# Reordering the second batch of an attention-and-MLP kernel: loads as k, q, v; k pooled apart from v; folded blocks 3 and 4 made inside its first product

## The chip, the cores and the metric

The kernel runs on one core of a Trainium2 chip. The metric is the device time of one execution in microseconds (us). The profile's span is 1.8 us shorter than that time (248.5 against 250.3 us for the kernel before). Engines are called by their names in the profile: PE is TensorE, DVE is VectorE, ACT is ScalarE, POOL is GpSimd, SP is SyncE; PEld is TensorE's weight loads, and a q behind a name (SPq, POOLq) is the engine's own queue of issues and waits. PSUM is the memory into which TensorE's products go; an *eviction* is the DVE or ACT instruction that takes a result out of it. A run of a program on one core is counted as fast unless it is over 1.5% above the fastest of its kernel.

## The reference

Batch 8, 8 heads of width 64, sequence 576, 32 memory slots, then a feed-forward layer of 512 to 2048 to 512. Cut to what matters:

```python
a   = softmax(phi, axis=2)                       # over the sequence
k_m = einsum('bhsm,bhsd->bhmd', a, k)            # "pooling": 32 rows per head
v_m = einsum('bhsm,bhsd->bhmd', a, v)
attn = softmax(q @ k_m.T / 8)                    # [576, 32] per head
x    = concat_heads(attn @ v_m)                  # [8, 576, 512]
xn   = (x - mean) / sqrt(var + 1e-6) * g_ln
out  = x + relu(xn @ w_ch1) @ w_ch2
```

## The kernel before

Batches are numbered 0 to 7; the "second batch" is batch 1. The kernel never multiplies x by w_ch1. It folds the pooled v into w_ch1, giving the *folded blocks* w1b (four blocks of 512 columns per batch), and multiplies those by the normalised attention Eh. In the text folded blocks are counted from 1 (block 3 is `a_w1b(b, 2)`), the 16 column blocks of the product from 0, as in the code. That multiplication is the *first product* (`mm1`). The *second product* (`mm2`) applies w_ch2.

```python
def kv_mm(b, ps, sl, js=range(4)):       # pooling: 2 x 4 x 9 small matmuls, k and v side by side
    for c in range(NS):
        for j in js:
            for g in range(2):
                nc.tensor.matmul(ps[32*j:32*(j+1), g, 0:D*(sl.stop-sl.start)],
                                 e[r:r+TS, c, j, :], kv[r:r+TS, j, sl, D*c:D*(c+1)], ...)

def a_w1b(b, n, part=None):              # folded block n
    ps = big([P, 2, 512], FP32, "w1b_ps")            # one of three double PSUM buffers
    ...                                              # 8 matmuls, 64*32 each
    for g in range(2):                               # two evictions on DVE, 128x512 fp32
        nc.vector.scalar_tensor_tensor(out=s["w1b"][:, g, fs], in0=m_sb[:, fs],
            scalar=s["rsum"][:, g:g+1], in1=ps[:, g, 0:N], op0=ALU.mult, op1=ALU.add)

def mm1(b, j0, j1):                      # first product; column block j needs folded block j // 4
    for j in range(j0, j1):
        h_ps = big([P, 2, 512], FP32, "h_ps")        # the same three buffers
        ...                                          # 4 matmuls of 288 columns
        if j % 3 or j == 0: nc.scalar.activation(out=dst, in_=h_ps[...], func=AF.Relu)
        else:               nc.vector.tensor_scalar(out=dst, in0=h_ps[...], ... op0=ALU.max)
```

The order of every engine's work is that of the Python text, as the timelines show (their lines: start, length, engine, line, operation, shapes, count, and in brackets the idle time before it with what ended it). The second batch's attention is interleaved with the second product of tiles 2 and 3 of the first pair of batches:

```python
    mm2(0, 2, 0, 8)
    a_kv(1)                              # k and v pooled together
    mm2(0, 2, 8, 12)
    a_tr(1)                              # transposes of pooled k and v
    a_qT(1, 0)                           # transposes of q
    a_w1b(1, 0)
    mm2(0, 2, 12, 16, finish=False)
    a_qT(1, 1)
    a_w1b(1, 1)
    a_sc(1)                              # scores
    mm2_out(0, 2)
    mm2(0, 3, 0, 4)
    a_w1b(1, 2)
    a_den(1)                             # denominators and Eh
    load(2); a_exp(2)
    mm2(0, 3, 4, 12)
    a_w1b(1, 3)
    mm2(0, 3, 12, 16, finish=False)
    a_vb(1)
    mm2_out(0, 3)
    ... # then, per batch: mm1(b, 0, 16), and the next batch's attention between mm2s
```

The softmax here doesn't subtract the row's maximum and nothing guards it: scores larger than these inputs give would overflow.

Of the kernel before, what the change touches and what calls it, by code (L numbers as in the profile page):

```python
# [9 lines left out]
FP32 = mybir.dt.float32  # L10
BF16 = mybir.dt.bfloat16
# [5 lines left out]
def kernel(  # L17
# [11 lines left out]
    nc = tc.nc  # L29

    B, H, S, D = q.shape
# [3 lines left out]
    P = 128  # L35
    TS = 64
    NS = S // TS
# [18 lines left out]
    def big(shape, dtype, name):  # L56
        return psum.tile(shape, dtype, name=name, tag="big", bufs=3)
# [16 lines left out]
    def rows(src, b):  # L74
        return src[b].rearrange("(j e) (p c) d -> (e p) j (c d)", e=2, p=TS)

    def halves(two):
        return (slice(0, 2), slice(2, 4)) if two else (slice(0, 4),)

    def load_kv(b):  # L80
        t = inp.tile([P, 4, 2, NS * D], BF16, name="kv_bf")
        for slot, src in ((0, k), (1, v)):
            for js in halves(b < 1):
                nc.gpsimd.dma_start(out=t[:, js, slot, :], in_=rows(src, b)[:, js, :])  # L84
        return t

    def load_q(b):
        t = inp.tile([P, 4, NP, P], BF16, name="q_bf")
        pad = nc.vector if b == 0 else nc.gpsimd
        pad.memset(t[:, :, NP - 1, D:], 0.0)  # L90
        for js in halves(b < 2):
            nc.gpsimd.dma_start(out=t.rearrange("p j n x -> p j (n x)")[:, js, 0:NS * D],  # L92
                                in_=rows(q, b)[:, js, :])
        return t
# [43 lines left out]
    for n in range(4):  # L138
        w2_load(n)
    phi1 = load_phi(1, nc.gpsimd)  # L140
    kv1 = load_kv(1)
    q1 = load_q(1)
    loaded[1] = (phi1, kv1, q1)

    g_bf = consts.tile([P, 4], BF16, name="g_bf")
# [94 lines left out]
    def a_kv(b):  # L240
        ps = big([P, 2, 512], FP32, "kv_ps")
        if b < 2:
            kv_sum(b, ps)
        else:

            for i in range(2):
                nc.tensor.matmul(ps[:, 0, P:P + 2], st8[b]["es"][:, i, :], ones8,
                                 start=(i == 0), stop=(i == 1))
        kv_mm(b, ps, slice(0, 2))
        k_out(b, ps, b < 2)  # L250
        v_out(b, ps[:, :, D:2 * D])
        rs_out(b, ps)

    def a_tr(b, k_part=True, v_part=True):
        s = st8[b]
        t_ps = big([P, 3, P], BF16, "kvT_ps")
        if k_part:
            kvT = att.tile([P, 3, P], BF16, name="kvT")
            s["kvT"] = kvT
            for g in range(2):  # L260
                nc.tensor.transpose(t_ps[:, g, :], s["k2"][:, g].rearrange("p a d -> p (a d)"), ident)
        kvT = s["kvT"]
        if v_part:
            nc.tensor.transpose(t_ps[:, 2, :], s["v2"].rearrange("p a d -> p (a d)"), ident)
        if k_part:
            nc.vector.tensor_copy(out=kvT[:, 0:2, :], in_=t_ps[:, 0:2, :])
        if v_part:
            nc.vector.tensor_tensor(out=kvT[:, 2, :].rearrange("p (j m) -> p j m", m=M),
                                    in0=t_ps[:, 2, :].rearrange("p (j m) -> p j m", m=M),
                                    in1=g_bf.unsqueeze(2).to_broadcast([P, 4, M]), op=ALU.mult)  # L270
            rsum = att.tile([P, 2], FP32, name="rsum")
            nc.vector.tensor_reduce(out=rsum, in_=s["v2"], axis=mybir.AxisListType.X, op=ALU.add)
            s["rsum"] = rsum

    def a_vb(b):
        s = st8[b]
        vb = att.tile([P, 2, 4, D], BF16, name="vb", bufs=3)
        for g in range(2):
            vsl = s["v2"][:, g, :].unsqueeze(1).to_broadcast([P, 4, D])
            eng = nc.vector if b < 2 else nc.gpsimd  # L280
            eng.tensor_tensor(out=vb[:, g], in0=vsl, in1=vmask, op=ALU.mult)  # L281
        s["vb"] = vb
# [91 lines left out]
    def a_w1b(b, n, part=None):  # L374
        s = st8[b]
        if n == 0 and part in (None, 0):
            s["w1b"] = att.tile([P, 2, F], BF16, name="w1b", bufs=1)
        ps = big([P, 2, 512], FP32, "w1b_ps")
        fs = slice(512 * n, 512 * (n + 1)) if part is None else W1C[part]
        N = fs.stop - fs.start  # L380
        for j in range(4):
            for g in range(2):
                r = 64 * g
                nc.tensor.matmul(  # L384
                    ps[32 * j:32 * (j + 1), g, 0:N], s["kvT"][r:r + 64, 2, 32 * j:32 * (j + 1)],
                    w1r[r:r + 64, j, fs], start=True, stop=True, tile_position=(r, 32 * j))
        for g in range(2):
            nc.vector.scalar_tensor_tensor(  # L388
                out=s["w1b"][:, g, fs], in0=m_sb[:, fs], scalar=s["rsum"][:, g:g + 1],
                in1=ps[:, g, 0:N], op0=ALU.mult, op1=ALU.add)  # L390


    pair = {}

    def mm1(b, j0, j1):
        s = st8[b]
        if b % 2 == 0 and j0 == 0:
            pair[b // 2] = moe.tile([P, JC, 2 * S], BF16, name="rT", bufs=1)
        rT = pair[b // 2]
        off = S * (b % 2)  # L400
        for j in range(j0, j1):
            h_ps = big([P, 2, 512], FP32, "h_ps")
            for g in range(2):
                for half in range(2):
                    nc.tensor.matmul(  # L405
                        h_ps[:, half, 0:HS], s["w1b"][:, g, P * j:P * (j + 1)],
                        s["Eh"][:, g, HS * half:HS * (half + 1)],
                        start=(g == 0), stop=(g == 1))
            dst = rT[:, j, off:off + S].rearrange("p (a x) -> p a x", a=2)
            if j % 3 or j == 0:  # L410
                nc.scalar.activation(out=dst, in_=h_ps[:, :, 0:HS], func=AF.Relu)  # L411
            else:
                nc.vector.tensor_scalar(out=dst, in0=h_ps[:, :, 0:HS], scalar1=0.0, scalar2=None,  # L413
                                        op0=ALU.max)
# [53 lines left out]
    def mm2(pr, t, j0, j1, ps=None, finish=True):  # L468
        rT = pair[pr]
        if j0 == 0:  # L470
            chs[(pr, t)] = one([P, C], FP32, "ch_ps") if ps is None else ps
        ch_ps = chs[(pr, t)]
        for j in range(j0, j1):
            nc.tensor.matmul(ch_ps, rT[:, j, P * t:P * (t + 1)], w2b[:, j, :],  # L474
                             start=(j == 0), stop=(j == JC - 1))
        if j1 == JC and finish:
            mm2_out(pr, t)

    def mm2_last(pr, t):

        x, rstd = xs[(pr, t)]
        for n in range(2):
            ps = big([P, 2, 512], FP32, "last_ps")
            cs = slice(256 * n, 256 * (n + 1))
            for j in range(JC):
                nc.tensor.matmul(ps[:, 0, 0:256], pair[pr][:, j, P * t:P * (t + 1)], w2b[:, j, cs],  # L486
                                 start=(j == 0), stop=(j == JC - 1))
            nc.vector.scalar_tensor_tensor(out=x[:, cs], in0=ps[:, 0, 0:256], scalar=rstd,
                                           in1=x[:, cs], op0=ALU.mult, op1=ALU.add)
            for u, queue in ((0, nc.sync), (1, nc.scalar)):  # L490
                lo = P * t + TS * u
                dst = out[2 * pr + lo // S].rearrange("(p c) x -> c p x", c=NS)
                queue.dma_start(out=dst[CO[lo % S // TS]][:, cs], in_=x[TS * u:TS * (u + 1), cs])

    def mm2_out(pr, t):
        ch_ps = chs[(pr, t)]
        x, rstd = xs[(pr, t)]
        nc.vector.scalar_tensor_tensor(out=x, in0=ch_ps, scalar=rstd, in1=x,  # L498
                                       op0=ALU.mult, op1=ALU.add)
        for u in range(2):  # L500
            lo = P * t + TS * u
            dst = out[2 * pr + lo // S].rearrange("(p c) x -> c p x", c=NS)
            nc.sync.dma_start(out=dst[CO[lo % S // TS]], in_=x[TS * u:TS * (u + 1), :])
# [44 lines left out]
    w1_mean(4)  # L548
    m_copy(4)
    a_w1b(0, 3)  # L550
    a_vb(0)
    mm1(0, 8, 16)

    x_tiles(0, [0, 1])
    x_tiles(0, [2, 3])
# [4 lines left out]
    a_exp(1)  # L560
    mm2(0, 0, 4, 16)
    mm2(0, 1, 4, 16)
    mm2(0, 2, 0, 8)
    a_kv(1)
    mm2(0, 2, 8, 12)
    a_tr(1)
    a_qT(1, 0)
    a_w1b(1, 0)
    mm2(0, 2, 12, 16, finish=False)
    a_qT(1, 1)  # L570
    a_w1b(1, 1)
    a_sc(1)
    mm2_out(0, 2)
    mm2(0, 3, 0, 4)
    a_w1b(1, 2)
    a_den(1)
    load(2)
    a_exp(2)
    mm2(0, 3, 4, 12)
    a_w1b(1, 3)  # L580
    mm2(0, 3, 12, 16, finish=False)
    a_vb(1)
    mm2_out(0, 3)

    a_qT(2, 0)
    late = []
    for b in range(1, B):
        pr, nb = b // 2, b + 1
        odd = b % 2
# [125 lines left out]
```

## Time and profile before

| | before |
|---|---|
| time, median of 3 runs | 251.05 us (250.95 to 251.22) |
| span of the profiled execution | 248.5 us (its time 250.3) |
| PE busy | 96% of the span |
| first product of batch 0, first to last matmul | 19.55 to 33.53 us |
| first product of batch 1 | 53.34 to 61.93 us |
| first product of each later batch | 8.12 us |
| last tile of the second product to the end of the span | 7.45 us |

The prediction shows the lines that carry the argument. Two more are needed as a yardstick, from the TensorE timeline (start, length, engine, line, operation, shapes, count, and in brackets the idle time before it with what ended it):

```profile
53.34 1.21 PE L405 MATMUL h_ps<-Eh,w1b 128*128 128x288 bf16 x8
54.79 7.14 PE L405 MATMUL h_ps<-Eh,w1b 128*128 128x288 bf16 x56 [0.25 <-ACT rT L411]
```

In the kernel before, batch 1's first product has one short wait and then runs 56 matmuls without a gap. The next work starts at 61.77, so the product takes 8.43 us from start to start (8.59 to the modelled end of its last matmul).

### The profile page before, as it was taken

How to read it: one execution, taken by the hardware profiler on the slowest of the kernel's cores; microseconds unless marked ns; L12 is line 12 of the kernel's file. 1: busy time of each engine (PE TensorE's matmuls, PEld its weight loads, DVE VectorE, ACT ScalarE, POOL GpSimd, SP SyncE). 2: the span in 40 equal slices, each digit the busy share in tenths (PEclk: the TensorE clock that was granted, in tenths of full speed). 3: DMA queues.
4: the chain of work that ended last, by engine and by line, in shares of the span. 5: the costliest groups of instructions: out<-in, count | busy, mean ns of one | idle time of the engine just before them, and what ended most of it. 6: DMA issues, size and time to landing. Idle time of an engine off the chain costs nothing.

```text
span 248.5 us, 5893 instructions
## 1 busy us (share of the span) xinstructions
PE 238.5 (96%) x2491; PEld 132.5 (53%) x2491; DVE 156.2 (63%) x304; ACT 130.0 (52%) x219; POOL 60.6 (24%) x100
## 2 busy tenths in 40 slices
PE   7879999999999999999999999999999999999993
PEld 2444555557544665467544774467444764476453
DVE  3246663785578646686569547785679538783641
ACT  3165572587463555736472646655680755465210
POOL 8643241032515402090206202170205011000000
PEclk9999999999999999999999999999999999999999
DMA  7999999998599899829975995539983302103133
GB/s 151 195 202 207 206 257 208 291 222 148 119 200 210 122 218 242 160 38 201 251 127 112 158 245 136 122 38 223 209 158 77 80 7 46 42 17 70 42 84 84
DMA packets 42450, 36.82 MB, mean 148 GB/s; under 512 B 17460, under 2 KB 37688, under 8 KB 42424
## 3 DMA queue, kind: packets, MB, share of 16 engines
q0 software_dynamic: 17776, 19.53, 46.9%
q1 hardware_dynamic: 24488, 16.79, 29.3%
q8 instruction: 19, 0.31, 0.5%
q10 hardware_dynamic: 160, 0.13, 0.2%
q14 instruction: 7, 0.06, 0.1%
HBM read 41.42 MB, written 9.44 MB: 205 GB/s over the span
## 4 chain that ended last, share of the span: by engine, by line
PE 88%; DMA 4%; DVE 2%; ACT 2%; POOL 1%; issue 1%; DVEq 0%; POOLq 0%
PE ch_ps L474 50%; PE h_ps L405 25%; DMA kv_bf<-in_v_dram 4%; PE w1b_ps L384 3%; PE kv_ps L210 2%; PE o_ps L435 2%; PE last_ps L486 1%; PE sc_ps L322 1%; PE m_ps L165 1%; ACT rT L411 1%; PE den_ps L353 1%; DVE w1b L388 1%; POOL q_bf L92 1%; ACT E_sb L327 1%; POOL kv_bf L84 1%
## 5 line engine op out<-in xcount | busy, mean ns | idle before, releaser
L474 PE MATMUL ch_ps<-w2b,rT 128*128 128x512 bf16 x560 | 128.4, 380 | 0.0
L474 PEld LDWEIGHTS <-rT 128*128 128x128 bf16 x560 | 52.0, 98 | 63.5 <-issue 6.5
L405 PE MATMUL h_ps<-Eh,w1b 128*128 128x288 bf16 x512 | 66.6, 286 | 1.3 <-ACT rT L411 1.2
L411 ACT ACTIVATE rT<-h_ps 128x576 bf16<-128x576 f32 x88 | 52.4, 648 | 28.7 <-PE h_ps L405 28.7
L405 PEld LDWEIGHTS <-w1b 128*128 128x128 bf16 x512 | 49.5, 97 | 18.3 <-issue 2.6
L388 DVE SCALAR_TENSOR_TENSOR w1b<-m_sb,rsum,w1b_ps 128x512 bf16<-128x512 f32 (+1 forms) x66 | 44.2, 726 | 9.6 <-PE w1b_ps L384 5.3
L413 DVE TENSOR_SCALAR rT<-h_ps 128x576 bf16<-128x576 f32 x40 | 30.3, 757 | 24.9 <-PE h_ps L405 24.3
L498 DVE SCALAR_TENSOR_TENSOR x_sb<-ch_ps,rstd,x_sb 128x512 f32<-128x512 f32 x35 | 26.1, 746 | 9.9 <-PE ch_ps L474 9.1
L454 DVE BATCH_NORM_STATS2 bst<-x_sb 128x6 f32<-128x512 f32 x36 | 24.4, 678 | 7.6 <-ACT x_sb L441 7.6
L441 ACT ACTIVATE x_sb<-o_ps 128x1024 f32<-128x1024 f32 (+1 forms) x20 | 17.5, 938 | 18.4 <-PE o_ps L435 18.4
L281 POOL TENSOR_TENSOR vb<-v,vmask 128x256 bf16<-128x256 bf16 x12 | 7.7, 663 | 60.1 <-DVE rs L237 60.1
L194 POOL TENSOR_TENSOR es<-e_sb 128x512 f32<-128x512 bf16 x6 | 6.9, 1156 | 62.9 <-ACT e_sb L187 62.9
L460 ACT ACTIVATE rstd<-mv,eps_sb 128x2 f32<-128x2 f32 (+1 forms) x20 | 5.9, 297 | 30.4 <-DVE mv L455 30.2
L327 ACT ACTIVATE E_sb<-sc_ps,rs 128x640 bf16<-128x640 f32 x16 | 11.8, 790 | 12.4 <-PE sc_ps L322 12.4
L369 DVE SCALAR_TENSOR_TENSOR Eh<-E_sb,rs,rden 128x576 bf16<-128x576 bf16 x16 | 12.4, 815 | 8.8 <-ACT rden L368 8.8
L384 PE MATMUL w1b_ps<-w1r,kvT 64*32 64x512 bf16 (+1 forms) x264 | 10.9, 374 | 0.0
L179 PE MATMUL w_ps<-fill 128*128 128x512 f32 (+1 forms) x16 | 9.4, 699 | 1.6 <-DVE fill L119 1.6
L227 DVE CAST k<-kv_ps 128x256 bf16<-128x256 f32 x7 | 3.0, 425 | 12.5 <-PE kv_ps L210 12.5
L187 ACT ACTIVATE e_sb<-phi_st 128x1152 bf16<-128x1152 f32 x8 | 9.2, 1151 | 2.6 <-DMA phi_st<-in_phi_dram 2.6
L368 ACT ACTIVATE rden<-rden 128x576 f32<-128x576 f32 x16 | 10.0, 672 | 0.1
L92 POOL DMA_DIRECT2D q_bf<-in_q_dram x10 | 7.6, 756 | 4.6 <-DMA w2b<-in_moe_w_ch_dram 1.8
L210 PE MATMUL kv_ps<-kv_bf,e_sb 64*32 64x128 bf16 (+1 forms) x648 | 7.4, 215 | 0.6 <-DMA kv_bf<-in_v_dram 0.3
(76 smaller groups left out, 151.3 us busy)
## 6 DMA issues: line engine op xcount, KB each, us to landing
out_dram<-x_sb SPq DMA_DIRECT2D x70, 128.0 KB, 2.8
kv_bf<-in_k_dram POOLq DMA_DIRECT2D x7, 576.0 KB, 6.1
kv_bf<-in_v_dram POOLq DMA_DIRECT2D x7, 576.0 KB, 9.2
phi_st<-in_phi_dram SPq DMA_DIRECT2D x6, 576.0 KB, 6.1
q_bf<-in_q_dram POOLq DMA_DIRECT2D x6, 576.0 KB, 13.9
w2b<-in_moe_w_ch_dram POOLq DMA_DIRECT2D x4, 512.0 KB, 17.7
w1r<-in_moe_w_ch_dram POOLq DMA_DIRECT2D x3, 512.0 KB, 13.8
q_bf<-in_q_dram POOLq DMA_DIRECT2D x4, 288.0 KB, 12.4
```

The lines of the kernel that those rows point to most:

```text
L210: nc.tensor.matmul(ps[32 * j:32 * (j + 1), g, 0:D * (sl.stop - sl.start)], e[r:r + TS, c, j, :], kv[r:r + TS, j, sl, D * c:D * (c + 1)], s ...
L327: nc.scalar.activation(out=E_[:, g].rearrange("p (a x) -> p a x", a=2), in_=sc[:, :, 0:HP], func=AF.Exp, scale=s["rs"][:, g:g + 1])
L369: nc.vector.scalar_tensor_tensor(out=Eh[:, g, :], in0=s["E"][:, g, 0:S], scalar=s["rs"][:, g:g + 1], in1=rd[:, g].rearrange("p a x -> p (a ...
L384: nc.tensor.matmul(ps[32 * j:32 * (j + 1), g, 0:N], s["kvT"][r:r + 64, 2, 32 * j:32 * (j + 1)], w1r[r:r + 64, j, fs], start=True, stop=Tru ...
L388: nc.vector.scalar_tensor_tensor(out=s["w1b"][:, g, fs], in0=m_sb[:, fs], scalar=s["rsum"][:, g:g + 1], in1=ps[:, g, 0:N], op0=ALU.mult, o ...
L405: nc.tensor.matmul(h_ps[:, half, 0:HS], s["w1b"][:, g, P * j:P * (j + 1)], s["Eh"][:, g, HS * half:HS * (half + 1)], start=(g == 0), stop= ...
L411: nc.scalar.activation(out=dst, in_=h_ps[:, :, 0:HS], func=AF.Relu)
L413: nc.vector.tensor_scalar(out=dst, in0=h_ps[:, :, 0:HS], scalar1=0.0, scalar2=None, op0=ALU.max)
L441: nc.scalar.activation(out=x[:, 0:n].rearrange("p i (u y) -> p i u y", u=2), in_=o_ps.rearrange("p u (i y) -> p i u y", i=2)[:, 0:n], func ...
L454: nc.vector.bn_stats(out=stt, in_=x)
L474: nc.tensor.matmul(ch_ps, rT[:, j, P * t:P * (t + 1)], w2b[:, j, :], start=(j == 0), stop=(j == JC - 1))
L498: nc.vector.scalar_tensor_tensor(out=x, in0=ch_ps, scalar=rstd, in1=x, op0=ALU.mult, op1=ALU.add)
```

## The change

Its intent: k and q are wanted first and v later, so the loads come in that order and k is pooled without waiting for v. TensorE should start the second batch earlier, and the two last folded blocks, which wait for v, are made where the first product has already begun. Four small parts come with it: another split of batch 0's ReLUs between ACT and DVE, a later `a_vb(0)`, batch 0's last output moved behind batch 1's first product, and a last tile cut 384+128 instead of 256+256. The core of the diff:

```diff
-    kv1 = load_kv(1)
+    kv1 = inp.tile([P, 4, 2, NS * D], BF16, name="kv_bf")
+    nc.gpsimd.dma_start(out=kv1[:, :, 0, :], in_=rows(k, 1))
     q1 = load_q(1)
+    for js in halves(True):
+        nc.gpsimd.dma_start(out=kv1[:, js, 1, :], in_=rows(v, 1)[:, js, :])
...
-            if j % 3 or j == 0:
+            if j % 3 != 1 if b == 0 else j % 3 or j == 0:
...
-        for n in range(2):                       # last tile: 256 + 256
+        for cs in (slice(0, 384), slice(384, 512)):
...
+    mm1(0, 8, 11)
     a_vb(0)
-    mm1(0, 8, 16)
+    mm1(0, 11, 16)
...                                               # second batch, now:
+    mm2(0, 2, 0, 4)
+    k_ps = big([P, 2, 512], FP32, "kv_ps")
+    kv_sum(1, k_ps); kv_mm(1, k_ps, slice(0, 1)); k_out(1, k_ps, True); rs_out(1, k_ps)
+    mm2(0, 2, 4, 7)
+    a_tr(1, v_part=False)
+    a_qT(1, 0)
+    mm2(0, 2, 7, 12)
+    a_qT(1, 1)
+    mm2(0, 2, 12, 16)
+    a_sc(1)
+    v_ps = big([P, 2, 512], FP32, "kv_ps")
+    kv_mm(1, v_ps, slice(1, 2), (0, 1))
+    mm2(0, 3, 0, 3)
+    kv_mm(1, v_ps, slice(1, 2), (2, 3)); v_out(1, v_ps[:, :, 0:D])
+    a_den(1, finish=False)
+    mm2(0, 3, 3, 5)
+    a_tr(1, k_part=False)
+    a_den2(1)                                     # Eh
+    load(2); a_exp(2)
+    mm2(0, 3, 5, 7);  a_w1b(1, 0)
+    mm2(0, 3, 7, 11); a_w1b(1, 1)
+    mm2(0, 3, 11, 16, finish=False)
+    # inside mm1(1): after four column blocks, after seven, after the end
+    late = [lambda: a_w1b(1, 2), blocks, lambda: mm2_out(0, 3)]   # blocks(): a_w1b(1, 3); a_vb(1)
```

More of the change, by code (lines that the diff above doesn't have):

```diff
@@ L481, in mm2_last @@
         x, rstd = xs[(pr, t)]
-        for n in range(2):
+        for cs in (slice(0, 384), slice(384, 512)):
             ps = big([P, 2, 512], FP32, "last_ps")
-            cs = slice(256 * n, 256 * (n + 1))
+            N = cs.stop - cs.start
             for j in range(JC):
-                nc.tensor.matmul(ps[:, 0, 0:256], pair[pr][:, j, P * t:P * (t + 1)], w2b[:, j, cs],
+                nc.tensor.matmul(ps[:, 0, 0:N], pair[pr][:, j, P * t:P * (t + 1)], w2b[:, j, cs],
                                  start=(j == 0), stop=(j == JC - 1))
-            nc.vector.scalar_tensor_tensor(out=x[:, cs], in0=ps[:, 0, 0:256], scalar=rstd,
+            nc.vector.scalar_tensor_tensor(out=x[:, cs], in0=ps[:, 0, 0:N], scalar=rstd,
                                            in1=x[:, cs], op0=ALU.mult, op1=ALU.add)
@@ L562, with blocks @@
     mm2(0, 1, 4, 16)
-    mm2(0, 2, 0, 8)
-    a_kv(1)
-    mm2(0, 2, 8, 12)
-    a_tr(1)
+    mm2(0, 2, 0, 4)
+    k_ps = big([P, 2, 512], FP32, "kv_ps")
+    kv_sum(1, k_ps)
+    kv_mm(1, k_ps, slice(0, 1))
+    k_out(1, k_ps, True)
+    rs_out(1, k_ps)
+    mm2(0, 2, 4, 7)
+    a_tr(1, v_part=False)
     a_qT(1, 0)
-    a_w1b(1, 0)
-    mm2(0, 2, 12, 16, finish=False)
+    mm2(0, 2, 7, 12)
     a_qT(1, 1)
-    a_w1b(1, 1)
+    mm2(0, 2, 12, 16)
     a_sc(1)
-    mm2_out(0, 2)
-    mm2(0, 3, 0, 4)
-    a_w1b(1, 2)
-    a_den(1)
+    v_ps = big([P, 2, 512], FP32, "kv_ps")
+    kv_mm(1, v_ps, slice(1, 2), (0, 1))
+    mm2(0, 3, 0, 3)
+    kv_mm(1, v_ps, slice(1, 2), (2, 3))
+    v_out(1, v_ps[:, :, 0:D])
+    a_den(1, finish=False)
+    mm2(0, 3, 3, 5)
+    a_tr(1, k_part=False)
+    a_den2(1)
     load(2)
     a_exp(2)
-    mm2(0, 3, 4, 12)
-    a_w1b(1, 3)
-    mm2(0, 3, 12, 16, finish=False)
-    a_vb(1)
-    mm2_out(0, 3)
+    mm2(0, 3, 5, 7)
+    a_w1b(1, 0)
+    mm2(0, 3, 7, 11)
+    a_w1b(1, 1)
+    mm2(0, 3, 11, 16, finish=False)
+    def blocks():
+        a_w1b(1, 3)
+        a_vb(1)
     a_qT(2, 0)
-    late = []
+    late = [lambda: a_w1b(1, 2), blocks, lambda: mm2_out(0, 3)]
     for b in range(1, B):
```

## The prediction

> **What bounds the kernel now.** I read the busy times first, then the chain that ended last, then the second batch's stretch by windows and timeline, because all large parts of the change lie there or just before it.
>
> From the page, the busy times and the chain by engine:
>
> ```profile
> PE 238.5 (96%) x2491; PEld 132.5 (53%) x2491; DVE 156.2 (63%) x304; ACT 130.0 (52%) x219; POOL 60.6 (24%) x100
> ...
> PE 88%; DMA 4%; DVE 2%; ACT 2%; POOL 1%; issue 1%; DVEq 0%; POOLq 0%
> ```
>
> TensorE is busy for 96% of the span and makes 88% of the chain. A change of order that removes no TensorE work can win back only its idle moments. The windows view puts the second batch between 34 and 62 us (columns: stretch, length, then busy time and count by engine):
>
> ```profile
> 34.13:42.78 8.65, 8.65 (x44) 3.93 (x42) 4.85 (x11) 3.76 (x7) 1.98 (x4) 1.00 1.19 236
> 42.78:53.34 10.56, 10.49 (x182) 5.52 (x181) 7.53 (x15) 6.88 (x10) 0.00 (x0) 1.00 1.17 257
> 53.34:61.77 8.43, 8.18 (x66) 6.22 (x65) 5.66 (x10) 6.53 (x12) 3.70 (x6) 1.00 0.91 175
> ```
>
> The first stretch is 40 products of 512 columns, so one costs 8.65/40 = 0.216 us. The second is the batch's attention between 24 more of them; the third is its first product (64 matmuls, ideally the 7.96 us that this takes in later batches in the chain view).
> The DVE timeline in the second and third stretch:
>
> ```profile
> 46.08 1.41 DVE L388 SCALAR_TENSOR_TENSOR w1b<-m_sb,rsum,w1b_ps 128x512 bf16<-128x512 f32 x2 [0.34 <-PE w1b_ps L384]
> ...
> 52.05 1.55 DVE L369 SCALAR_TENSOR_TENSOR Eh<-E_sb,rs,rden 128x576 bf16<-128x576 bf16 x2 [0.70 <-ACT rden L368]
> 53.52 1.40 DVE L388 SCALAR_TENSOR_TENSOR w1b<-m_sb,rsum,w1b_ps 128x512 bf16<-128x512 f32 x2
> ...
> 57.47 0.76 DVE L413 TENSOR_SCALAR rT<-h_ps 128x576 bf16<-128x576 f32 x1 [0.74 <-PE h_ps L405]
> ```
>
> Three of the four folded blocks (w1b, 1.4 us of DVE each) are evicted before Eh is ready at 53.6, while TensorE multiplies something else. Once the product runs, DVE has idle time before every ReLU (0.74 us). This is what the change gives up.
>
> [...]in the PE timeline 36 pooling matmuls of 64 columns make room for the next work after 0.38 us (10.90 to 11.28), 72 of 128 columns after 0.74 (43.07 to 43.81), thus 10 ns each at either width. [...]here eight block matmuls take 0.35 us and their eviction 1.4. [...]
>
> **The change part by part.**
>
> *Load order.* Landing = issue plus time to landing in the DMA view: k at 20.6+19.2 = 39.8, v at 23.15+19.6 = 42.7, q at 44.5 and 46.3. TensorE uses k and v at 42.8 and q at 44.85 and 46.8, so everything comes just in time and no wait shows. With k, q, v and the same bytes I expect k 39.8, q about 41.5 and 43.3, v about 44.8 and 46.3. The new order uses them at about 41.9, 43.5, 45.3, 47.3 and 48.4: no wait either. Gain by itself zero; it makes room for an earlier start.
>
> *k pooled apart from v.* 72 more matmuls at 10 ns: +0.75 us of TensorE. Nine stretches of the second product stand where six stood; a group of four takes 0.97 instead of 4 x 0.216 = 0.87, so 3 x 0.1 = +0.3. Removed: the stall around the scores (0.4 for the copy of q: 0.87 instead of 0.47) and perhaps 0.15 at the denominators. Two block products (0.52; 24 matmuls, three blocks, take 0.77 in a later batch) move behind the point at which the first product starts. Sum up to that point: 0.75+0.3-0.55-0.52, about 0. TensorE would be ready for the first product at 53.3 to 53.4, as before, with 0.3 of gain from batch 0 already used.
>
> *ReLU split and late vb in batch 0.* I walked the blocks with 0.52 us each, ACT 0.65, DVE 0.76. Up to 30 us the fold of the weights' mean (ACT copy, then two DVE evictions) sets the pace and the new split changes nothing; the bubble at 31.38 goes away. Gain 0.3 us.
>
> *Blocks 3 and 4 inside the first product.* This is the expensive part. DVE now evicts no block before Eh. TensorE's order up to the denominators is 51 products (11.0) plus pooling 1.8, transposes 1.3, scores 0.5, denominators 0.5 and 0.5 for interruptions from 33.8: 49.4. Two ACT logarithms and the first exponential give Eh its start near 51.05. Then DVE runs without a gap, in its built order: Eh 1.5, blocks 1 and 2 at 1.3 each (one every 0.655) to 55.2, ReLU of column block 3 to 56.6 (its matmul waits for block 2's PSUM), block 3 to 57.9, ReLU 6 to 58.7, block 4 to 60.0, vb to 60.4, ReLU 9 to 61.2. TensorE waits: for block 1 at the start (first half done 53.3, second 53.95), for PSUM around column blocks 2 and 3, 7, and 10 (until 60.2), and for ReLU 9 before 12 (61.35, because each PSUM tile has its place in the built program and block 12 takes that of 9). Four blocks remain: 61.3 + 4 x 0.52 = 63.4, against 61.77. Cost +1.6 us, with the 0.3 of batch 0 and all of the above in it.
>
> *Last tile 384+128 instead of 256+256.* TensorE: 16 x 0.163 + 16 x 0.057 (the rate of ten 128-column transposes, 0.57) = 3.5, as now 3.51. The last DVE step falls from 0.48 (256 columns) to some 0.35, and the last rows are half as long: -0.15.
>
> Sum: +1.6 - 0.15 = +1.45; I take +1.35 because a part of the bubbles may overlap better than in a walk by hand. Later batches keep their order and should keep their times.
>
> **The rivals.**
> *A: the author's intent holds.* Then TensorE, not DVE, sets the end of the first product. For it: DVE has slack in the page (63%) and idles 0.74 before each ReLU. Against it: that slack, four gaps of 0.74 = 3 us, has to take two or three further blocks of 1.3 each, plus the two that now come after Eh. Even then the best case is small: about 1 us of stall in 42.8 to 53.3 and 0.47 in the product can vanish, 0.3 in batch 0 and 0.15 at the end, less 1.05 of added TensorE work: 250.2.
> *B: a transfer becomes the wait.* The halves of v land last, at about 46.3, and batch 2's inputs are one issue later in the queue. A v half late by 2 us would stall the pooling before the denominators and push Eh by as much: 253.5 to 254. Against: the queue moved a steady stream in this stretch and v is wanted 2 us after its estimated landing.
> *C: DVE bound as in the main theory but worse*, since in-order DVE puts block evictions in front of ReLUs that TensorE's three PSUM buffers wait for: each such bubble of 0.5 more, four times, gives 254.
>
> **Range and chances.** The main walk gives 251.05 + 1.35 = 252.4 us. The low side is a DVE cost of a third of mine (+0.5, less 0.6 of gains); the high side is B or C in part. 2% is 5 us, and no rival reaches it in either direction: the whole stall to be won is under 2 us, and the whole DVE work moved is 5.6 us, of which most stays beside TensorE.
>
> **What would show each step.** Right: in the DVE timeline a row of 1.5 (Eh) near 51, directly followed by about 2.7 us of w1b for two blocks and no idle time until ReLU 9; the first product of batch 1 taking 9.5 to 10.5 us instead of 8.43, with TensorE waits named DVE w1b or DVE rT; its start within 0.5 us of 53.3; pooling in two groups of 0.75 us each with no DMA before them; the product of batch 0 ending 0.2 to 0.4 earlier than 33.46; batches 2 to 7 alike. Wrong: a wait of kv_ps on v's DMA (rival B), a first product of batch 1 under 9 us (rival A), or a time under 250.9, which would mean that DVE found its slack. If the head before 20 us moves, I have overlooked something, since no part of the change touches it.

In the kernel before's groups by form and its waits: DVE takes 743 ns to evict 128x512 fp32 (mean of the 62 of that size), and TensorE waits five times for an ACT ReLU before h_ps, 1.2 us in all. The 0.163 us for 384 columns can be read as an estimate: midway between the 0.216 us for 512 and the 3.51/32 = 0.110 us for 256.

## The result, and the profile after

The changed kernel took 252.68 us in the median of 4 runs (252.55 to 253.11), against 251.0 us (250.94 to 251.22) for the kernel before. The ratio is 1.0068, with a 95% interval of 1.0051 to 1.0086: within 2%, and clearly slower. A ratio here is the mean time of one kernel's fast runs over that of the other's of the same rounds, so it is not quite the ratio of the medians.

The busy times and the chain by engine of the changed kernel:

```profile
PE 240.7 (96%) x2563; PEld 132.6 (53%) x2563; DVE 156.4 (62%) x304; ACT 129.8 (52%) x219; POOL 61.1 (24%) x101
...
PE 78%; DMA 9%; DVE 6%; ACT 3%; POOL 1%; issue 1%; SPq 0%; DVEq 0%; POOLq 0%
```

TensorE has 72 matmuls more, the split pooling. Its share of the chain fell from 88% to 78%, because the chain now runs through DVE evictions and through one transfer of 14.17 us; TensorE still worked beside most of that, as its 96% shows. The spans differ by 2.28 us. Cut at the starts and ends of the first products, which the TensorE timeline shows, the difference lies here:

| stretch | before | after | difference |
|---|---|---|---|
| start of the span to the first 512-column product of batch 0's mean fold | 20.69 | 20.55 | -0.14 |
| from there to the end of batch 0's first product | 12.84 | 12.43 | -0.41 |
| to the start of batch 1's first product | 19.81 | 19.75 | -0.06 |
| batch 1's first product | 8.59 | 10.67 | +2.08 |
| its end to the start of batch 2's first product | 21.30 | 21.42 | +0.12 |
| end of batch 2's first product to the start of batch 3's | 17.31 | 18.15 | +0.84 |
| batch 3's first product to the last tile | 132.39 | 132.38 | 0 |
| last tile to the end | 7.45 | 7.31 | -0.14 |

The sum is +2.3. The medians of the timed runs differ by 1.7 only. The profiled execution of before (250.3 us) was faster than all its timed runs; what made it so is not shown.

**The first product of batch 1.** The DVE timeline of the changed kernel:

```profile
50.47 1.55 DVE L373 SCALAR_TENSOR_TENSOR Eh<-E_sb,rs,rden 128x576 bf16<-128x576 bf16 x2 [0.58 <-ACT rden L372]
51.94 2.72 DVE L392 SCALAR_TENSOR_TENSOR w1b<-m_sb,rsum,w1b_ps 128x512 bf16<-128x512 f32 x4
55.73 0.76 DVE L417 TENSOR_SCALAR rT<-h_ps 128x576 bf16<-128x576 f32 x1 [1.08 <-PE h_ps L409]
56.40 1.40 DVE L392 SCALAR_TENSOR_TENSOR w1b<-m_sb,rsum,w1b_ps 128x512 bf16<-128x512 f32 x2
58.05 0.76 DVE L417 TENSOR_SCALAR rT<-h_ps 128x576 bf16<-128x576 f32 x1 [0.25 <-PE h_ps L409]
58.73 1.39 DVE L392 SCALAR_TENSOR_TENSOR w1b<-m_sb,rsum,w1b_ps 128x512 bf16<-128x512 f32 x2
```

And TensorE in the same stretch:

```profile
52.73 0.42 PE L409 MATMUL h_ps<-Eh,w1b 128*128 128x288 bf16 x2
53.40 0.91 PE L409 MATMUL h_ps<-Eh,w1b 128*128 128x288 bf16 x6 [0.24 <-DVE w1b L392]
54.55 1.14 PE L409 MATMUL h_ps<-Eh,w1b 128*128 128x288 bf16 x8 [0.25 <-ACT rT L415]
55.62 0.41 PE L388 MATMUL w1b_ps<-w1r,kvT 64*32 64x512 bf16 x8
55.96 1.23 PE L409 MATMUL h_ps<-Eh,w1b 128*128 128x288 bf16 x8
57.37 0.65 PE L409 MATMUL h_ps<-Eh,w1b 128*128 128x288 bf16 x4 [0.18 <-ACT rT L415]
57.95 0.41 PE L388 MATMUL w1b_ps<-w1r,kvT 64*32 64x512 bf16 x8
58.29 1.23 PE L409 MATMUL h_ps<-Eh,w1b 128*128 128x288 bf16 x8
59.69 3.71 PE L409 MATMUL h_ps<-Eh,w1b 128*128 128x288 bf16 x28 [0.17 <-ACT rT L415]
```

All four folded blocks are evicted after Eh; none was before it. The pieces of the product can be read from start to start, with 0.124 us for one matmul (7.96/64, the ideal that the prediction quotes). The first two matmuls take 0.67 instead of 0.25: they wait for the second half of block 1 (+0.42). The next six take 1.15 instead of 0.75 (+0.40); a wait of this size stood in the kernel before too. Two block products take 0.34 each (+0.68); they used to stand before the product. Beside each of them a group of eight takes 1.40 instead of 1.00 (2 x 0.41 extra), and every such pause ends with an ACT ReLU. In that stretch each block holds one of the three PSUM buffers from its matmuls until DVE has evicted it (block 3 from 55.62 to 57.80, block 4 from 57.95 to 60.12), and the column blocks alternate between the other two (column block 6 starts at 57.37, behind a ReLU on ACT and before block 3's buffer is free).

The 0.68 us of block products are moved work, not lost time: they left the stretch in front of the product, and the split pooling took their place there (0.81 + 0.43 + 0.38 = 1.62 us against 0.74 in the kernel before), so that stretch stayed at 19.75.

**The stretch between batches 2 and 3.** The waits view of the changed kernel has a line that the kernel before has not, and the chain in order of time shows the transfer behind it (start, length):

```profile
PE sc_ps L326 <- DMA qT<-q_bf: 0.8, 1, 0.8
```

```profile
86.17 14.17 DMA qT<-q_bf
100.48 0.47 PE sc_ps L326 x16
```

Batch 3's scores wait 0.8 us for its transposed q. No part of the change touches batch 3.

### The profile page after: what moved, and what is told of

It is laid out like the page before. It is cut to its first block, busy times and chain, and to the rows that moved or that the text cites. A ratio compares the mean times of both kernels' runs of the same rounds, so it can differ in the third digit from the quotient of the medians.

```text
span 250.8 us, 6038 instructions
## 1 busy us (share of the span) xinstructions
PE 240.7 (96%) x2563; PEld 132.6 (53%) x2563; DVE 156.4 (62%) x304; ACT 129.8 (52%) x219; POOL 61.1 (24%) x101
## 3 DMA queue, kind: packets, MB, share of 16 engines
HBM read 41.42 MB, written 9.44 MB: 203 GB/s over the span
## 4 chain that ended last, share of the span: by engine, by line
PE 78%; DMA 9%; DVE 6%; ACT 3%; POOL 1%; issue 1%; SPq 0%; DVEq 0%; POOLq 0%
PE ch_ps L478 44%; PE h_ps L409 21%; DMA qT<-q_bf 6%; DMA kv_bf<-in_v_dram 3%; DVE w1b L392 3%; PE w1b_ps L388 3%; PE kv_ps L214 2%; PE last_ps L490 1%; PE o_ps L439 1%; ACT rT L415 1%; PE sc_ps L326 1%; PE m_ps L169 1%; DVE Eh L373 1%; PE den_ps L357 1%; POOL q_bf L92 1%
## 5 line engine op out<-in xcount | busy, mean ns | idle before, releaser
L409 PE MATMUL h_ps<-Eh,w1b 128*128 128x288 bf16 x512 | 67.4, 286 | 2.1 <-ACT rT L415 1.3
L183 PE MATMUL w_ps<-fill 128*128 128x512 f32 (+1 forms) x16 | 10.3, 762 | 1.6 <-DVE fill L119 1.6
L214 PE MATMUL kv_ps<-kv_bf,e_sb 64*32 64x128 bf16 (+1 forms) x720 | 8.5, 210 | 0.5 <-DVE rs L241 0.3
## 6 DMA issues: line engine op xcount, KB each, us to landing
w1r<-in_moe_w_ch_dram POOLq DMA_DIRECT2D x3, 512.0 KB, 14.2
```

The lines of the kernel that those rows point to most:

```text
L214: nc.tensor.matmul(ps[32 * j:32 * (j + 1), g, 0:D * (sl.stop - sl.start)], e[r:r + TS, c, j, :], kv[r:r + TS, j, sl, D * c:D * (c + 1)], s ...
L409: nc.tensor.matmul(h_ps[:, half, 0:HS], s["w1b"][:, g, P * j:P * (j + 1)], s["Eh"][:, g, HS * half:HS * (half + 1)], start=(g == 0), stop= ...
```

## The experiments

Twelve runs of eleven kernels were made (small_parts twice), in three groups on two chips. small_parts_2 was meant for another chip than small_parts, as its expectation says; the record has both on chip 6. The runs of the kernel before that shared these chips spread from 250.1 to 253.5 us, so their intervals are wide (0.3% to 0.7% to each side), and differences of a few tenths are read from the stretches of the profile, which repeat to about 0.02 us where nothing waits for a transfer (8.59 and 8.60, 10.66 and 10.67, 17.31 in the table). The exception is the head: in the twelve profiles with an unaltered head, batch 0's first product starts anywhere from 18.99 to 21.40 us. That spreads the spans of the profiles; of the other runs there is no profile.

| kernel | time, us | before, same chip | ratio (95%) | batch 0 end to batch 1 start | batch 1's product | batch 2 to 3 |
|---|---|---|---|---|---|---|
| before (first profile) | 251.0 | | | 19.81 | 8.59 | 17.31 |
| changed | 252.68 | 251.0 | 1.0068 (1.0051 to 1.0086) | 19.75 | 10.67 | 18.15 |
| small_parts | 250.59 | 250.66 | 0.9987 (0.9954 to 1.002) | 19.78 | 8.60 | 17.31 |
| small_parts_2 | 250.43 | 250.86 | 0.9973 (0.9933 to 1.0013) | 20.43 | 8.60 | 17.31 |
| second_batch | 253.56 | 250.66 | 1.0108 (1.0076 to 1.014) | 19.70 | 10.66 | 18.15 |
| order_alone | 255.39 | 250.66 | 1.0169 (1.0121 to 1.0217) | 22.62 | 8.60 | 17.31 |
| q_early | 253.42 | 250.66 | 1.0091 (1.0048 to 1.0135) | 19.75 | 10.66 | 17.42 |
| v_early | 251.97 | 250.6 | 1.004 (0.9985 to 1.0094) | 19.95 | 9.59 | 18.15 |
| phi_first | 252.93 | 250.6 | 1.0081 (1.0029 to 1.0133) | 19.76 | 10.66 | 18.25 |
| blocks_before | 254.28 | 250.6 | 1.0142 (1.0074 to 1.0211) | 21.73 | 9.44 | 18.15 |
| relu_act | 252.92 | 250.6 | 1.0094 (1.0028 to 1.0159) | 19.76 | 10.60 | 18.63 |
| pad_before | 252.2 | 250.86 | 1.0034 (0.9972 to 1.0096) | 19.81 | 8.60 | 18.06 |
| pad_after | 253.83 | 250.86 | 1.0108 (1.0055 to 1.0161) | 20.30 | 10.66 | 17.31 |
| one_banks | 252.83 | 250.86 | 1.0077 (1.0023 to 1.0132) | 19.75 | 10.48 | 18.04 |

All outputs are right.

### The small parts alone, twice

Edit to the kernel before: the ReLU condition, `a_vb(0)` behind `mm1(0, 8, 11)`, and the 384+128 cut, as in the diff above; nothing else.

> The kernel before with the two small parts alone: the ReLU split and the later vb in batch 0, and the last tile as 384+128. My theory (parts add up; each small part is worth what its stage shows in the profile after): 0.4 us less in batch 0's first product, 0.15 less at the end, so 250.45 us against 251.0, ratio 0.998. Rival: batch 0's gain is eaten because v of the second batch lands only at 42.7 and its pooling then waits up to 0.3 us for it, so 250.75. Second rival: the 0.4 us was the start of that one profile and not the split: 250.85.

> The kernel before with the two small parts once more, on another chip, since the first chip's runs spread by 1%. If the stages in the profile tell the truth (0.4 us in batch 0's first product, 0.15 at the end, all else equal): ratio 0.998 and 0.5 us less than before. Rival: v's landing takes back most of it, ratio 0.9995.

The stretch to the end of batch 0's first product is 12.43 us in both, as in the changed kernel (12.84 before), and the end takes 7.31 in both instead of 7.45. So the parts are worth 0.41 and 0.14 us in their stages. Whether that reaches the time is not settled: both ratios lie below 1, both intervals contain 1. The second profile shows how it can be lost. There batch 0 ended early (33.27), and batch 1 then waited for its loads (TensorE timeline):

```profile
45.25 0.73 PE L304 MATMUL qT_ps<-ident,q_bf 128*128 128x128 bf16 x10 [0.30 <-DMA q_bf<-in_q_dram]
```

With the old load order q landed at 45.20 and 47.12, and the way to batch 1's product took 20.43 us instead of 19.81. The rival, which named v, was right in kind. v landed at 42.97 and its pooling began at 43.01, 0.51 us after the sums in front of it instead of 0.29, so some 0.2 of the 0.62 is v's; the larger part is q's. In the kernel before, the second batch starts when its loads land, and an earlier start in batch 0 can be lost there.

### The second batch alone

The changed kernel with the ReLU split, `a_vb(0)` and the last cut put back.

> The changed kernel without the two small parts, thus load order, split pooling and late blocks alone. My theory: the whole loss sits here, +1.68 measured plus the 0.55 that the small parts give back: 253.2 us, ratio 1.009; batch 1's first product takes about 10.6 us in the profile. Rival: the small parts did nothing, 252.7 as the changed kernel.

It took 253.56 us (1.0108). The product takes 10.66 us, and the +0.84 between batches 2 and 3 is there again. The whole loss sits in the second batch's parts.

### The load order alone

```diff
 # kernel before, plus the new order of the loads; a_kv(1) as it was
-    kv1 = load_kv(1)
-    q1 = load_q(1)
+    kv1 = inp.tile(...); k in one DMA; q1 = load_q(1); v in two halves
```

> The kernel before with the load order k, q, v alone; k and v are still pooled together at 42.8 us. My theory: the last half of v lands near 46.2 as in the changed kernel, so TensorE waits 3.4 us on the DMA of v there, less some 0.4 us of the wait for the copied q that then lies ready: 254 us, ratio 1.012. Rival: the queue is not the limit and the order costs nothing, 251.0.

```profile
44.10 0.24 PE L214 MATMUL kv_ps<-kv_bf,e_sb 64*32 64x128 bf16 x4 [0.56 <-DMA kv_bf<-in_v_dram]
46.32 0.76 PE L214 MATMUL kv_ps<-kv_bf,e_sb 64*32 64x128 bf16 x68 [1.99 <-DMA kv_bf<-in_v_dram]
```

TensorE waits for both halves of v (2.55 us in all; 3.4 were expected), and batch 1's product starts 2.8 us later after batch 0 (22.62 against 19.81); the time was 255.39 us, 1.4 above what was expected. The profiled run was the fastest (253.46); of the other three, with a granted clock of 0.99 and up to 2.9 us longer, there is no profile. The order by itself is a loss, so pooling k apart is needed to pay for it, and it does pay: with both, that stretch is 19.75.

### The transpose of q issued earlier

```diff
-            mm2_out(pr, t[3])
             if b == 1:
                 a_qT(nb + 1, 0)
+            mm2_out(pr, t[3])
```

> The changed kernel, with the transposing transfer of q for batch 3 put in front of the last output of pair 0 on SyncE instead of behind it, so it is issued near 82.5 (when q has landed) instead of 86.2. My theory: the 0.8 us wait of sc_ps on that transfer in the profile after is a real knock-on of the later first product and goes away: about 251.9 us, 0.8 less than the changed kernel. Rival: that wait belongs to the one profiled execution or the transfer gets no faster, since it shares the engines with the loads of batch 4 either way: 252.7, no change; the transfer would then land near 100 again.

The stretch between batches 2 and 3 fell from 18.15 to 17.42 us, so the wait is real and its cause is the landing of that transfer. The transfer itself got no faster (14.8 us from issue to landing, 14.2 in the changed kernel); it was issued 1.1 us before batch 2's product instead of 1.35 after it. The time did not show the gain: 253.42 us, in a set of runs from 251.99 to 254.79. The expected 251.9 was missed.

### Evictions in front of Eh

```diff
     v_ps = big([P, 2, 512], FP32, "kv_ps")
-    kv_mm(1, v_ps, slice(1, 2), (0, 1)); mm2(0, 3, 0, 3); kv_mm(1, v_ps, slice(1, 2), (2, 3)); v_out(...)
+    kv_mm(1, v_ps, slice(1, 2)); v_out(...); mm2(0, 3, 0, 3); a_tr(1, k_part=False)
     a_den(1, finish=False)
+    a_w1b(1, 0)                                  # block 1 before Eh
     a_den2(1)
     ...                                          # blocks 2 and 3 between mm2s; only block 4 in the product
-    late = [lambda: a_w1b(1, 2), blocks, lambda: mm2_out(0, 3)]
+    late = [lambda: a_w1b(1, 3), lambda: a_vb(1), lambda: mm2_out(0, 3)]
```

> The changed kernel with all of v pooled at once behind the scores, and the evictions reordered: block 1 before Eh, blocks 2 and 3 before the first product, only block 4 inside it. Nothing is removed; the same evictions stand earlier in DVE's order. My theory (the first product waits for DVE, which starts its block evictions only after Eh): batch 1's first product takes about 9.2 us instead of 10.67 and ends 1.3 us earlier relative to the end of batch 0's, so 251.4 us or ratio 1.002 against before. Rival: the first product is long because TensorE makes the blocks there and PSUM has three buffers; then only the one block taken out (0.35 us) is won: about 252.3.

```profile
49.53 1.41 DVE L392 SCALAR_TENSOR_TENSOR w1b<-m_sb,rsum,w1b_ps 128x512 bf16<-128x512 f32 x2 [0.56 <-PE w1b_ps L388]
50.85 1.54 DVE L373 SCALAR_TENSOR_TENSOR Eh<-E_sb,rs,rden 128x576 bf16<-128x576 bf16 x2
52.31 2.72 DVE L392 SCALAR_TENSOR_TENSOR w1b<-m_sb,rsum,w1b_ps 128x512 bf16<-128x512 f32 x4
```

Block 1's eviction now fills DVE's idle time before Eh. The product takes 9.59 us; together with the way to it, 29.54 us against 30.42 of the changed kernel and 28.40 of before. This order gives back 0.9 us with the same work, more than the 0.35 of the rival and less than the 1.3 that I expected. It has the lowest median of the versions with the new load order, 251.97 us (1.004; its interval overlaps theirs), and is still not ahead of the kernel before.

### Blocks 3 and 4 in front of the product

```diff
     mm2(0, 3, 11, 16, finish=False)
+    a_w1b(1, 2); a_w1b(1, 3); a_vb(1)
-    late = [lambda: a_w1b(1, 2), blocks, lambda: mm2_out(0, 3)]
+    late = [lambda: None, lambda: None, lambda: mm2_out(0, 3)]
```

> The changed kernel with blocks 3 and 4 and vb put in front of the first product again, nothing else. My theory (DVE's queue, not the place of the blocks, makes the loss): no gain. TensorE then waits for PSUM until DVE has evicted them; the first product starts near 54.7 and ends near 63.9 instead of 63.4 in the profile, thus up to 0.5 us slower, 252.7 to 253.2. Rival (making blocks inside the product costs it the 2 us): the product takes 8.6 us again and the time falls to about 251.

```profile
53.30 0.41 PE L388 MATMUL w1b_ps<-w1r,kvT 64*32 64x512 bf16 x8 [0.39 <-DVE w1b L392]
54.62 0.66 PE L409 MATMUL h_ps<-Eh,w1b 128*128 128x288 bf16 x4 [0.91 <-DVE w1b L392]
56.02 1.14 PE L409 MATMUL h_ps<-Eh,w1b 128*128 128x288 bf16 x8 [0.74 <-ACT rT L415]
```

The product is shorter (9.44 us) and begins later (21.73): 31.17 together, 0.75 us worse than in the changed kernel. The time, 254.28 us, is above the expected 252.7 to 253.2; the profiled run took 253.23, two others 255 at a granted clock of 0.993. Making the blocks inside the product is not what costs; as long as all four are evicted after Eh, it is the better place.

### Two ReLUs moved from DVE to ACT

```diff
-            if j % 3 != 1 if b == 0 else j % 3 or j == 0:
+            if j % 3 != 1 if b == 0 else j % 3 or j == 0 or (b == 1 and j < 9):
```

> The changed kernel with the ReLUs of column blocks 3 and 6 of batch 1 on ScalarE instead of VectorE, which takes 1.5 us off DVE in the stretch where I say that it is the limit and adds 1.3 us to ACT. My theory: blocks 3 and 4 are evicted 0.3 and 0.9 us earlier and batch 1's first product takes 9.7 to 10 us instead of 10.67. Rival: DVE isn't the limit there, ACT's ReLUs release PSUM (six waits of PE name ACT): the product stays at 10.7 or gets longer.

```profile
56.30 1.41 DVE L392 SCALAR_TENSOR_TENSOR w1b<-m_sb,rsum,w1b_ps 128x512 bf16<-128x512 f32 x2 [1.45 <-PE w1b_ps L388]
57.56 0.65 PE L409 MATMUL h_ps<-Eh,w1b 128*128 128x288 bf16 x4 [0.23 <-ACT rT L415]
```

The product stayed at 10.60 us. The rival was right here: taking 1.5 us of DVE work out of the product wins 0.07 us. Counted from the start of the product, blocks 3 and 4 are evicted 0.30 and 0.31 us earlier (expected 0.3 and 0.9). DVE now stands ready for block 3, which still keeps its buffer until 57.71, and TensorE still waits for a ReLU on ACT. The queue of ReLUs on DVE is thus not what TensorE waits for; the 1.4 us of each block's own eviction were not removed. That the stretch between batches 2 and 3 is longer here than anywhere (18.63) is not explained.

### Blocks 3 and 4 in other PSUM banks

```diff
-        ps = big([P, 2, 512], FP32, "w1b_ps")
+        if b == 1 and n >= 2:
+            pss = [one([P, 512], FP32, "w1b_ps") for _ in range(2)]
+        else: ps = big(...); pss = [ps[:, g, :] for g in range(2)]
...
-    mm2(0, 3, 11, 16, finish=False)
+    mm2(0, 3, 11, 16)                             # its output again in front of the product
```

> The changed kernel, with blocks 3 and 4 built in the two single PSUM banks that are free there instead of in one of the product's three double buffers, and batch 0's last output back in front of the product (it has to free one of those banks). DVE has the same work in the same stretch, and 0.75 us more before the first ReLU. Buffer theory (relu_act left the product at 10.6: what it waits for is PSUM, since each block keeps one of three buffers for 1.5 to 2 us and the product alternates between two): batch 1's first product takes about 9.5 us instead of 10.67. DVE theory in its old form (DVE's queue limits): it stays above 10.3, or gets longer.

```profile
56.50 1.64 PE L413 MATMUL h_ps<-Eh,w1b 128*128 128x288 bf16 x12
58.07 0.72 PE L392 MATMUL w1b_ps<-w1r,kvT 64*32 64x512 bf16 x8
58.73 2.62 PE L413 MATMUL h_ps<-Eh,w1b 128*128 128x288 bf16 x20
61.60 2.15 PE L413 MATMUL h_ps<-Eh,w1b 128*128 128x288 bf16 x16 [0.25 <-ACT rT L419]
```

The pause beside the first block is gone: 12 matmuls take 1.57 us from start to start, against 1.49 ideal. But block 4 then takes 0.66 us instead of 0.34, since its two banks are still being evicted (DVE has block 3 from 56.94 to 58.34), and a new pause of 0.4 stands before the last 16. The product took 10.48 us, not 9.5; by the number the DVE theory (above 10.3) was right. So the buffers do make the pause beside block 3, and with it gone others of nearly the same sum appear: 0.32 us for block 4's own banks, which is a want of PSUM again, and the 0.4, which the profile puts down to a ReLU on ACT, while DVE's ReLU of column block 9 stood behind block 4 and vb until 61.39. How much of the last is DVE's is not shown. This run does not separate the two limits, and one that gives each block its own banks and also frees DVE was not made.

This run also shows where the +0.12 us after the product comes from: with batch 0's output back in front, the stretch to batch 2's product is 21.30 again; in every kernel with the late output it is 21.41 or 21.42.

### What delays batch 3's q: the load behind the late output?

```diff
-    late = [lambda: a_w1b(1, 2), blocks, lambda: mm2_out(0, 3)]
+    late = [lambda: a_w1b(1, 2), blocks, lambda: (phis.update({3: load_phi(3)}), mm2_out(0, 3))]
```

> The changed kernel, with the load of phi for batch 3 issued on SyncE in front of batch 0's last output (made late by the change) instead of behind it, so near 61.5 instead of 66.1. My theory of the 0.8 us wait of the scores on the transposed q of batch 3: the late output holds up this load in SyncE's order, its 0.6 MB then share the engines with the loads of batch 3, these land over 1 us later, and so do all behind them up to the transpose. Then the stretch between the first products of batches 2 and 3 falls from 18.15 back to 17.3 to 17.5 us; 252.0 us. Rival: the late output itself or the later batch 3 loads do it, and the stretch stays at 18.15; 252.7.

The load was issued at 61.19, as wanted, and the stretch stayed at 18.25 us. That theory fell. one_banks, where the output itself is early again, still has 18.04, so the late output does not do it either.

### What delays batch 3's q: the place of an instruction packet

The page lists a DMA queue of kind "instruction" whose packets carry 16 KB (0.31 MB in 19 packets in the kernel before). In all kernels with the 144 added entries in TensorE's program (72 matmuls with their weight loads), one such packet falls 8.2 to 8.7 us after the start of batch 2's first product, in the middle of the transfer (in the changed kernel at 93.01, where it takes 0.96 us: 54.3% of 16 engines over 0.11 us); in the others there is none until 12.3 (in the kernel before just under 95.6). The page of the kernel before counts 19 of these packets, for 2491 matmuls with as many weight loads (4982 entries), and that of the changed kernel 20, for 5126: if they carry TensorE's program, one holds about 260 entries (an estimate from these counts: 4982/19 = 262, 5126/20 = 256). pad_after adds 112 entries, which with the 144 of the change make 256, close to this estimate. To test the theory, TensorE's program alone is made longer, in the head, where TensorE multiplies dummies anyway:

```diff
-    warm(3)
+    warm(1)
+    for _ in range(72):                           # pad_after: 56
+        nc.tensor.matmul(pad_ps[:, 0:32], blk, blk[:, 0:32], start=True, stop=True)
```

> The kernel before with two of its three first warm-up products replaced by 72 small dummy matmuls, so that TensorE's program is longer by the same 144 entries (weight load and matmul) as the changed one, and nothing else differs. New theory of the 0.8 us wait of the scores on the transposed q of batch 3: phi_first did not remove it, and in every kernel with the 144 added entries a 16 KB instruction packet falls 8.2 to 8.7 us after the start of batch 2's first product, in the middle of batch 4's loads and of that transpose, where kernels without them have none until 12.3[...]. Then this kernel shows the packet near 8.2 and the stretch between the first products of batches 2 and 3 at about 18.1 us; time about 251.5. Rival: the wait comes from the late output or the later batch 1, and the stretch stays at 17.31; 250.7 to 251.

> The changed kernel with two of its three first warm-up products replaced by 56 small dummy matmuls, thus 112 more entries in TensorE's program[...]. Instruction-packet theory: no packet between 0 and 12 us after the start of batch 2's first product except the small one near 3, the stretch between the first products of batches 2 and 3 back at 17.3 to 17.4 us, and the time 0.8 us below the changed kernel, about 251.9. Rival (late output, later batch 1): 18.15 again and 252.7.

The added entries are a little fewer than these texts say. The two warm-up products taken out were four matmuls with their weight loads (the page has 16 for eight such products): the count of weight loads rises from 2491 to 2559 in pad_before and from 2563 to 2615 in pad_after, thus by 136 and 104 entries net instead of 144 and 112. The packets fell nearly where they were wanted all the same, at 8.9 us in pad_before and at 12.3 in pad_after.

The DMA view of the 12 us from the start of batch 2's first product (the queues' packets, bytes and share of the engines, then the issues with their time to landing; other lines of the view are left out, and the kernel before has no instruction queue in it). The kernel before, 83.23 to 95.23 us:

```profile
q1 hardware_dynamic: 2424, 0.84, 33.0%
issues: line engine op xcount, KB each, median us to landing
q_bf<-in_q_dram POOLq DMA_DIRECT2D x1, 576.0 KB, 11.8
qT<-q_bf SPq DMA_TRANSPOSE x1, 13.1
```

The same kernel with 72 dummy matmuls (pad_before), 84.51 to 96.51 us:

```profile
GB/s 146 192 215 200 215 207 192 180 150 173 196 192 192 196 271 271 257 252 273 276 213 193 205 195 192 206 189 201 202 243 186 185 178 125 9 73 243 190 154 120
q8 instruction: 1, 0.02, 0.5%
q_bf<-in_q_dram POOLq DMA_DIRECT2D x1, 576.0 KB, 12.8
qT<-q_bf SPq DMA_TRANSPOSE x1, 14.1
```

And the changed kernel with 56 dummies (pad_after), 88.09 to 100.09 us:

```profile
q14 instruction: 1, 0.01, 0.2%
q_bf<-in_q_dram POOLq DMA_DIRECT2D x1, 576.0 KB, 11.9
qT<-q_bf SPq DMA_TRANSPOSE x1, 13.2
```

Before has no instruction packet there, and the transpose lands after 13.1 us. The longer program puts a 16 KB packet there, and both the load of q and the transpose land 1.0 us later; TensorE's wait appears (0.7 us) and the stretch becomes 18.06. In the changed kernel 104 further entries, so 248 in all with its own 144, take the 16 KB packet away again (the one left is the 8 KB kind, q14 with 0.06 MB in 8 packets, which the changed kernel has too), and the stretch is 17.31. Both came out as expected, with no edit in batches 1 to 3. That the packet's place decides is shown. How it does so is not: the profile does not say which of the 16 engines carried the packet. What the GB/s row (40 slices of 0.3 us) adds is that all transfers together fall to 125, 9 and 73 GB/s from 9.9 us on, just as the packet ends (8.91 to 9.86), while the kernel before has no slice under 138 in its window. The changed kernel shows the same (84, 16 and 9 GB/s from 9.0 us on). So nearly the whole flow stops, not one engine's share of it; the loss is some 0.6 us of transfer at 200 GB/s (an estimate from this row).

In time the two runs show less. pad_before: 252.2 us, expected 251.5, interval across 1. pad_after: 253.83 us, expected 251.9, a miss: its head was altered and its batch 0 started at 22.30 in the profile, the latest of all, with a granted clock of 0.987. Its way to batch 1's product is also 0.55 us longer (20.30), all of it in the pooling of v's first half, where TensorE pauses for what the profile calls "issue".

## Why the prediction was right or wrong

The direction and the size hold: 252.4 predicted, 252.68 measured, between the 250.9 under which the text calls itself wrong and the 253.5 to 254 of its rivals B and C. Point by point:

- **Load order: right.** I expected k 39.8, q 41.5 and 43.3, v 44.8 and 46.3. They landed at 39.4, 40.9, 42.3, 44.3 and 46.2. TensorE waited for none of them, and order_alone shows what the order costs when v is still wanted early.
- **k apart from v, sum about 0: right.** The stretch from batch 0's product to batch 1's is 19.75 us, 19.81 before.
- **Batch 0, gain 0.3: right in kind, undersized.** The split is worth 0.41 us (12.84 to 12.43, the same in every kernel that has it); 0.14 more of that profile came from its head, which the change does not touch. Batch 1's product began at 52.73, not at 53.3 to 53.4. A part of that is a slip in the working: its sum of about 0, with the 0.3 of batch 0 that it says is used, gives 53.0 and not 53.3.
- **Blocks inside the product, end at 63.4: right in size and in most of the waits, wrong in what limits.** Eh began at 50.47 (expected 51.05), two blocks followed it for 2.72 us without a gap, and TensorE waited for block 1's second half and then for PSUM, as said (in front of column blocks 2, 6 and 9; 2 and 3, 7 and 10 were named). The step that failed is "then DVE runs without a gap, in its built order ... ReLU 9 to 61.2": DVE stood idle 1.08 us before ReLU 3 and 0.25 before ReLU 6, waiting for TensorE. (The prediction's own times leave 0.6 before ReLU 3, from 55.2 to the 56.6 at which 0.76 us of ReLU end.) TensorE's pauses named ACT's ReLUs, because a block held the third buffer; the wait for ReLU 9, which was to set the end, cost under 0.1 us, for the last 28 matmuls took 3.55 us from start to start, against 3.48 ideal. The predicted end, 63.4, agrees with the modelled 63.40 because two errors cancel: the product began 0.6 us earlier than predicted and took as much longer. Start to start it took 10.51 us, just past the "9.5 to 10.5" that was to show the step right.

  relu_act (10.60) shows that DVE's queue of ReLUs is not the limit; one_banks (10.48) shows that a block's hold on a buffer makes a pause, but not how much of the product the two limits make together: that stays open. What holds is the part that v_early and blocks_before agree on: in the order of the changed kernel all four evictions come after Eh, and the product meets them. Putting one eviction in front of Eh and building one more block ahead of the product gave 0.9 us back; building blocks 3 and 4 ahead of it without that made it worse.
- **Last tile, 0.15: right** (0.14).
- **"Later batches keep their order and should keep their times": wrong.** They lost 0.96 us in the profile, which no step of the sum had. 0.84 of it is the wait for batch 3's transposed q, caused by the length of TensorE's program and not by any order in it, as pad_before and pad_after show; 0.12 goes with the late output. I had counted the 144 added entries as TensorE time (0.75 us) and as nothing else.

The closeness of 252.4 is thus partly luck. In the pair of profiles the difference is 2.28 us, not 1.35: +1.47 up to the end of batch 1's product (+1.6 predicted), the unforeseen 0.96, and -0.14 at the end. The medians of the timed runs differ by 1.7 only. Rival A failed: the product of the changed kernel never came near 9 us. (The idle 0.74 us that it counts on stood before four of DVE's five ReLUs there, as its sum has it, not before every one.) Rival B (a late v) did not occur. Rival C (evictions that keep PSUM from the column blocks) was nearest in kind and too large: two pauses of 0.41 us beside blocks 3 and 4, not four of 0.5.

No version here was shown to beat the kernel before. The small parts come nearest, 0.55 us better in their stages and unclear in time.

## What to carry to other kernels

When a late input feeds evictions on an engine that works in the order of the text, as DVE did here, ask which of them used to fill that engine's idle time before the critical step, and where they will stand afterwards: here three evictions, 4.2 us of DVE work that had stood before that step and beside other work of TensorE, moved behind it and met the product. Before blaming the place of such work, try it elsewhere; before blaming one limit (the engine, the buffers), take each away alone, because two can stand behind each other. And when a stretch that the change does not touch moves by most of a microsecond, look for what shares its transfers, the program's own instruction packets included (here one of 16 KB went with 0.7 to 0.8 us of TensorE); a few dummy instructions are a cheap test.
